# Experts 4 to 7 of a top-1 routed layer in one pass each, by programs of 33 widths

## The chip, the cores and the metric

The kernel runs on one core of one Trainium2 chip. The metric is the device time of one execution in microseconds (us). All arithmetic of the products is in float32.

## The reference

A state-space scan gives 3072 tokens of 256 values; a router sends each token to the expert with the greatest logit, and the expert's two products are scaled by the softmax weight of that logit. Cut to what matters:

```python
x = attn_out.transpose(0, 2, 1, 3).reshape(3072, 256)   # scan over 4 x 8 heads, 768 steps
logits = x @ w_gate                                     # 8 experts
expert_idx = np.argmax(logits, axis=1)
probs = softmax(logits)
gate_w = probs[np.arange(N), expert_idx]
for e in range(8):
    mask = expert_idx == e
    h = np.maximum(x[mask] @ w1[e], 0.0)                # 256 -> 1024
    out[mask] = gate_w[mask, None] * (h @ w2[e])        # 1024 -> 256
```

With the inputs of this case the experts get 372, 343, 418, 417, 336, 365, 415 and 406 tokens.

## The kernel before, in words

**First part.** The scan runs over 24 tiles of 128 tokens. Each tile's rows (values, logits, token number: W = 265 numbers) are kept, and groups of tiles (RGS) are ranked: by counts and a triangular product, every token gets a place in its expert's region of x_hbm, a buffer in HBM. place (L553) scatters a tile to its places with an indirect DMA on GpSimd's queue. Tiles 0 to 16 are placed during the scan. Tiles 17 to 23, the last group, are ranked after it and get places from 256 on at least, so that the first 256 places of an expert may be read before the last group is known. empty (L190) writes zero rows, with a token number that is out of range, behind the tokens of the first groups.

**Second part.** Expert e has two weight matrices of 1 MB each (w_sb). Its first pass handles places 0 to 255: a_load (L596) fetches the rows from x_hbm; halves (L651, L653) splits the float32 words in two planes of 16 bits and turns them with a transposing DMA; words (L658) puts the turned planes together on VectorE into xT; m_h (L685) makes h in eight blocks, each with a ReLU by ScalarE into hT; m_y (L720) makes the result for two tiles of 128 tokens with hT as the stationary operand, and put (L703 by ScalarE, L705 by VectorE) scales it by the gate into yo, which an indirect DMA (L711, GpSimd) sends to its tokens in the output. TensorE's order is h of expert 0, h of 1, y of 0, h of 2, y of 1, and so on, one expert apart.

**What is left of an expert**, its places from 256, is done in pairs of experts: b_load (L606, L609) fetches a full tile of each and half a tile that both share. A Switch with five branches does h for 128 to 192 places according to the greater count of the pair, and m_half (L731) the shared half tile where one is needed. TensorE and ScalarE take the branch by a number that over computes from the counts; switch_hint names the target some time ahead.

**Order.** The program of the second part is recorded in a manual schedule: on each engine the instructions stand in the order in which the Python code emits them. VectorE, ScalarE and GpSimd each take them from one sequence. All fetches of rows and weights, all emptyings and all transposing DMAs are issued by SP from one sequence too: an issue whose wait isn't over holds all behind it. Weights of expert e + 2 are issued in the middle of expert e's first product, after the turn of expert e + 2. Placements and result sends are on GpSimd's queue. Buffers come from rotating pools: y_ps has two PSUM buffers, h_ps four, yo three, hT three.

A general path (If more > 0) serves inputs whose counts go over the places; it isn't taken here.

Of the kernel before, what the change touches and what calls it, by code (L numbers as in the profile page):

```python
# [24 lines left out]
NT = NP * NC  # L25
# [12 lines left out]
TA = CA // 128  # L38
NK = -(-(N - CAP) // 128)
NR = N + 128  # L40
# [4 lines left out]
def ssd_then_moe(ctx, tc, x, ad_in, az_in, B, BT, CT, w_gate, w1, w2, out):  # L45
# [30 lines left out]
    zrows = consts.tile([112, CAP // 112, W], FP32, name="zrows")  # L76
# [13 lines left out]
    nk = route.tile([128, 2 * E + 1 + E // 2], I32, name="nk")  # L90
# [50 lines left out]
    def empty_consts():  # L141

        z = sm.tile([128, 1], FP32, name="zero")
        nc.gpsimd.memset(z, 0.0)
        none_i = sm.tile([112, CAP // 112], I32, name="none_i")
        nc.gpsimd.iota(none_i, pattern=[[0, CAP // 112]], base=N, channel_multiplier=0)
        nc.scalar.copy(zrows, bc(z[0:112, 0:1, None], list(zrows.shape)))
        nc.gpsimd.tensor_copy(zrows[:, :, TOK].bitcast(I32), none_i)
# [37 lines left out]
    def empty(e):  # L186
# [3 lines left out]
        d = nc.sync.dma_start(out=x_hbm[ds(r, CAP), :].rearrange("(p c) w -> p c w", c=CAP // 112), in_=zrows)  # L190
        tc.declare_no_dep(d.ins, group="pa", reason="these rows lie behind the first pass's tokens")
        tc.declare_no_dep(d.ins, group="la", reason="another expert's rows")
        tc.add_to_no_dep_group("fl", d.ins)

# [82 lines left out]
    def load_w(e, uu=(0, 1)):  # L277
        for u in uu:
            nc.sync.dma_start(out=w_sb[e][u], in_=(w1, w2)[u][e])
# [254 lines left out]
    def rank(g):  # L534
# [11 lines left out]
        if g == GA - 1:  # L546
            nc.vector.tensor_tensor(out=row2, in0=rt_p[g][0:1, n], in1=base_f[0:1], op=ALU.add)

            nc.vector.scalar_tensor_tensor(out=base2, in0=rt_p[g][:, n], scalar=float(CA), in1=base_f,
                                           op0=ALU.max, op1=ALU.add)  # L550
# [16 lines left out]
    def over(tb, pp):  # L567
# [6 lines left out]
        nc.vector.tensor_scalar(out=ov, in0=cn, scalar1=float(127 - CAP), scalar2=0.0, op0=ALU.add, op1=ALU.max)  # L574
# [5 lines left out]
        nc.vector.tensor_copy(nk[:, E + 1:2 * E + 1], cn)  # L580

        ml = tb.tile([128, E // 2], FP32, name="ml")
        nc.vector.tensor_reduce(ml, cn.rearrange("p (b i) -> p b i", i=2), axis=AX, op=ALU.max)
        nc.vector.tensor_scalar(out=ml, in0=ml, scalar1=float(15 - CA - 128), scalar2=0.0, op0=ALU.add, op1=ALU.max)
        nc.vector.tensor_scalar(out=ml, in0=ml, scalar1=64.0, scalar2=None, op0=ALU.min)
        cl = nk[:, 2 * E + 1:]
        nc.vector.tensor_copy(cl, ml)
        nc.vector.tensor_scalar(out=cl, in0=cl, scalar1=4, scalar2=None, op0=ALU.logical_shift_right)
# [3 lines left out]
    pr = [dict() for _ in range(E // 2)]  # L592
# [8 lines left out]
    def b_load(v, mo):  # L601
        xs = ea.tile([128, TA, W], FP32, name="xs", bufs=4)
        xh = mo.tile([128, 1, W], FP32, name="xh", bufs=4)
# [8 lines left out]
    def gate_in(xs, n):  # L612

        lg = xs[:, :, 128:HB]
        mx = ea.tile([128, TA], FP32, name="gmx", bufs=2)[:, 0:n]
        nc.vector.tensor_reduce(mx, lg, axis=AX, op=ALU.max)
        sub = ea.tile([128, TA, E], FP32, name="gsub", bufs=2)[:, 0:n]
# [3 lines left out]
    def gate_out(sub, n):  # L621
        nc.scalar.activation(sub, sub, func=ACT.Exp)
        gt = ea.tile([128, TA], FP32, name="gate", bufs=5)[:, 0:n]
# [11 lines left out]
    def new_xT():  # L635
        return ea.tile([128, KT, CA], FP32, name="xT", bufs=3)
# [8 lines left out]
    def halves(tiles):  # L645
        n = len(tiles)
        pl = ea.tile([128, TA + 1, 2, KT, 128], U16, name="pl", bufs=2)[:, 0:n]
# [4 lines left out]
        tt = ea.tile([128, TA + 1, 2, KT, 128], U16, name="plT", bufs=2)[:, 0:n]  # L652
# [7 lines left out]
    def next_halves(i):  # L660

        if i < E:
            ex[i]["tt"] = halves([ex[i]["xs"][:, t] for t in range(TA)])
        elif i - E < E // 2:
            r = pr[i - E]
            r["tt"] = halves([r["xs"][:, 0], r["xs"][:, 1], r["xh"][:, 0]])

    def a_words(e):
        ex[e]["xT"] = new_xT()
        for i in range(TA):  # L670
# [9 lines left out]
    def up(xT, w, f, n, pp, step=CA):  # L680
        p = pp.tile([128, 512], FP32, name="h_ps", tag="h", bufs=4)
        for i in range(0, n, step):
            for t in range(KT):
                c = t * F + f * 128
                nc.tensor.matmul(p[:, i:min(i + step, n)], lhsT=w[:, c:c + 128], rhs=xT[:, t, i:min(i + step, n)],  # L685
# [347 lines left out]
```

## Time and profile before

| | us |
|---|---|
| median of 3 runs | 271.21 (270.74 to 272.68) |
| the profiled execution's own time | 271.81 |
| its span, first to last instruction | 270.0 |
| TensorE busy | 252.9 |
| VectorE, ScalarE, GpSimd busy | 110.7, 104.5, 87.0 |
| first product of expert 0 starts | 83.20 |
| mean granted TensorE clock | 0.992 |

PE is TensorE's products, PEld its weight loads, DVE VectorE, ACT ScalarE, POOL GpSimd; SPq is the issuing of DMAs by SP. L685 is a line of the kernel before. The slices divide the span in 40 equal parts of 6.75 us; a digit is the busy share in tenths. In the chain, an entry is a start, a length and the work; x32 counts TensorE's records, of which a float32 product has two. In timelines, what stands in brackets is how long the engine had been idle and what ended it. Idle time of an engine other than the one that sets the end costs nothing by itself.

The kernel moved 43.57 MB by DMA, 36.32 of them on the queue that SP issues to, 6.41 on GpSimd's.

### The profile page before, as it was taken

Reading aid. Unit: us, or ns where it says so; the run is one execution under the profiler, and the core shown is the slowest. Engines: PE = TensorE matmul, PEld = TensorE weight load, DVE = VectorE, ACT = ScalarE, POOL = GpSimd, SP = SyncE. Lnnn points to the kernel's source line nnn. Section 1 sums busy time; section 2 is a strip of 40 time slices with the busy share of each in tenths; the row PEclk is TensorE's granted clock in tenths of the full one; section 3 lists DMA queues with packets and bytes.
Section 4 is the critical chain, followed back from the end, with each engine's and each line's share of the span. In section 5 each row is a group of like instructions: output and inputs, shape, how many; then the busy total and the mean of one; then the engine's idle time right before and its main releaser. Section 6 shows DMA issues by size and latency. Waiting matters only on the chain.

```text
span 270.0 us, 7603 instructions
## 1 busy us (share of the span) xinstructions
PE 252.9 (94%) x3044; PEld 213.7 (79%) x3067; DVE 110.7 (41%) x358; ACT 104.5 (39%) x304; POOL 87.0 (32%) x171
## 2 busy tenths in 40 slices
PE   8799898999997999999999999999999999999990
PEld 2577677677776888888888888888998978989770
DVE  4889887888854240421211111233225115321010
ACT  6958574655543423223232323141050520604200
POOL 5666875866720002025504120202211102121021
PEclk9999999999999999999999999999999999999996
DMA  6956767671434899949695959533330601401010
GB/s 182 374 172 171 228 199 236 165 247 51 135 118 101 212 367 310 384 177 294 236 256 202 279 199 335 130 91 78 103 85 9 94 4 30 90 6 40 2 35 28
DMA packets 29715, 43.57 MB, mean 161 GB/s; under 512 B 16203, under 2 KB 19917, under 8 KB 27984
## 3 DMA queue, kind: packets, MB, share of 16 engines
q1 hardware_dynamic: 27152, 36.32, 45.4%
q0 software_dynamic: 2496, 6.41, 7.1%
q8 instruction: 36, 0.59, 0.9%
q14 instruction: 31, 0.25, 0.3%
HBM read 29.10 MB, written 10.73 MB: 147 GB/s over the span
## 4 chain that ended last, share of the span: by engine, by line
PE 82%; DVE 5%; DMA 4%; issue 4%; POOL 2%; ACT 1%; POOLq 0%; ACTq 0%; DVEq 0%
PE h_ps L685 33%; PE y_ps L720 30%; PE y L176 5%; PE rows_ps L176 4%; PE g L176 3%; PE A L176 3%; PE yh_ps L731 3%; DVE L L359 2%; DMA x_hbm<-rows,pos 1%; DMA xs<-x_hbm 1%; DMA az<-in_az_dram 1%; DMA ct<-in_CT_dram 1%; DVE M L386 1%; PE rank L176 1%; DVE S L431 1%
## 5 line engine op out<-in xcount | busy, mean ns | idle before, releaser
L685 PE MATMUL h_ps<-xT,w 128*128 128x256 f32 (+3 forms) x516 | 90.3, 334 | 0.6 <-ACT xT L641 0.5
L685 PEld LDWEIGHTS h_ps<-xT,w 128*128 128x128 f32 x516 | 81.3, 190 | 8.2 <-ACT xT L641 0.7
L720 PE MATMUL y_ps<-w,hT 128*128 128x256 f32 x384 | 84.9, 380 | 0.0
L720 PEld LDWEIGHTS y_ps<-w,hT 128*128 128x128 f32 x384 | 72.6, 190 | 10.5 <-issue 0.8
L696 ACT ACTIVATE hT<-h_ps 128x256 f32<-128x256 f32 (+3 forms) x128 | 43.3, 339 | 60.8 <-PE h_ps L685 53.1
L711 POOL DMA_INDIRECT out_dram<-yo,xs x24 | 23.7, 988 | 91.1 <-ACT yo L703 64.7
L553 POOL DMA_INDIRECT x_hbm<-rows,pos x24 | 24.4, 1015 | 20.6 <-DMA x_hbm<-zrows 13.3
L359 DVE TENSOR_TENSOR_SCAN L<-abc,ident 128x512 f32<-128x512 f32 x24 | 29.1, 1213 | 0.0
L651 DVE COPY pl<-xs 128x256 uint16<-128x256 uint16 x44 | 10.4, 298 | 43.8 <-DMA xs<-x_hbm 43.7
L658 DVE COPY xT<-plT 128x512 uint16<-128x512 uint16 (+1 forms) x30 | 10.6, 415 | 33.6 <-DMA plT<-pl 27.8
L703 ACT ACTIVATE yo<-y_ps,gate 128x256 f32<-128x256 f32 x14 | 6.6, 474 | 39.4 <-PE y_ps L720 24.5
L386 DVE TENSOR_TENSOR M<-g,L 128x512 f32<-128x512 f32 x24 | 16.5, 687 | 5.6 <-PE g L176 5.1
L176 PE MATMUL rows_ps<-turn,yT 128*128 128x136 f32 x96 | 15.4, 283 | 3.5 <-issue 2.7
L705 DVE TENSOR_SCALAR yo<-y_ps,gate 128x256 f32<-128x256 f32 x10 | 4.8, 482 | 29.3 <-PE y_ps L720 29.3
L176 PE MATMUL g<-ctm,bt 32*64 32x128 f32 x384 | 16.3, 280 | 0.5 <-ACT ctm L293 0.4
L176 PEld LDWEIGHTS rows_ps<-turn,yT 128*128 128x128 f32 x96 | 14.5, 192 | 1.3 <-issue 0.4
L711 POOL DMA_INDIRECT out_dram<-yh,xh x4 | 3.9, 978 | 35.7 <-ACT yh L733 23.9
L470 ACT COPY rows<-rows_ps 128x264 f32<-128x264 f32 x24 | 9.1, 380 | 13.5 <-PE rows_ps L176 10.9
L176 PE MATMUL y<-M,xn 64*32 64x64 f32 x768 | 12.9, 223 | 1.2 <-issue 1.2
L457 ACT COPY yT<-y 128x256 f32<-128x256 f32 x24 | 8.9, 372 | 12.2 <-PE y L176 10.2
L176 PEld LDWEIGHTS g<-ctm,bt 32*64 32x64 f32 x384 | 10.4, 131 | 3.2 <-ACT ctm L293 0.9
L366 POOL TENSOR_TENSOR bs<-bn,L 128x128 f32<-128x128 f32 x22 | 9.0, 410 | 11.1 <-DVE L L359 10.0
(132 smaller groups left out, 203.3 us busy)
## 6 DMA issues: line engine op xcount, KB each, us to landing
w<-in_w_dram SPq DMA_DIRECT2D x13, 1024.0 KB
x_hbm<-zrows SPq DMA_DIRECT2D x8, 463.8 KB
xn<-in_x_dram SPq DMA_DIRECT2D x12, 256.0 KB
w<-in_w_dram SPq DMA_DIRECT2D x12, 256.0 KB
xs<-x_hbm SPq DMA_DIRECT2D x8, 265.0 KB
ct<-in_CT_dram SPq DMA_DIRECT2D x6, 256.0 KB
bt<-in_BT_dram SPq DMA_DIRECT2D x6, 256.0 KB
bn<-in_B_dram SPq DMA_DIRECT2D x6, 256.0 KB
```

Of the source, the lines that this page charges most:

```text
L176: i = nc.tensor.matmul(out, lhsT=lhsT, rhs=rhs, **kw)
L359: nc.vector.tensor_tensor_scan(out=s["L"].rearrange("p h i -> p (h i)"), data0=s["abc"], data1=ident8.rearrange("p h i -> p (h i)"), initi ...
L366: nc.gpsimd.tensor_tensor(out=bs[n % 2], in0=gr[n // CG]["B"][:, n % CG].rearrange("p (h m) -> p h m", h=8), in1=bc(st[n]["L"][:, :, CH - ...
L386: nc.vector.tensor_tensor(out=s["M"].rearrange("p (s v u) i -> p s v (u i)", s=2, v=2), in0=s["g"][:, :, 0:256].rearrange("p v (s f) -> p ...
L470: nc.scalar.copy(out=rt[g][:, k - R0[g], 0:DM + E], in_=p)
L553: s_ = nc.gpsimd.indirect_dma_start(out=x_hbm[:, :], out_offset=bass.IndirectOffsetOnAxis(ap=pos[:, k:k + 1], axis=0), in_=rt[grp[k]][:, k ...
L651: nc.vector.tensor_copy(pl[:, i, :, t], f[:, :, HB * t:HB * t + 128])
L658: nc.vector.tensor_copy(xT.bitcast(U16).rearrange("p t (j c) -> p c t j", c=2), tt)
L685: nc.tensor.matmul(p[:, i:min(i + step, n)], lhsT=w[:, c:c + 128], rhs=xT[:, t, i:min(i + step, n)], start=(t == 0), stop=(t == KT - 1))
L696: nc.scalar.activation(hT[:, f, 0:n], p, func=ACT.Relu)
L711: s_ = nc.gpsimd.indirect_dma_start(out=out[:, :], out_offset=bass.IndirectOffsetOnAxis(ap=xs[:, TOK:TOK + 1].bitcast(I32), axis=0), in_=y ...
L720: nc.tensor.matmul(p, lhsT=hT[:, f], rhs=w_sb[e][1][:, f * DM:f * DM + DM], start=(f == 0), stop=(f == FT - 1))
```

## The change

Experts 0 to 3 keep a first pass of 256 places and pairs for the rest (EP = 4). Experts 4 to 7 are done in one pass over up to 512 places (CP = 512): a Switch with 33 branches does exactly 256 + 8c places (m_one). In it the second product has w2 as the stationary operand and hT as the moving one, so that the result comes out turned (yTp); turn_back splits it in planes, turns it with a transposing DMA, and put_back puts the words together, scales them and sends four tiles per expert.

So that a program's expert has all its tokens, the last group is ranked, counted and placed during the first product of expert 0 (late); experts 3 to 7 are emptied behind all of their tokens, after the count (empty_last), experts 0 to 2 before it as till now. p_load fetches 512 rows of an expert and waits for all placements and emptyings.

TensorE's order becomes: h of 0, h of 1, y of 0, y of 1, six of eight blocks of h of 2, program of 4, the other two blocks, one tile of y of 2, program of 5, the other tile, two blocks of h of 3, program of 6, the other six blocks, program of 7, y of 3, pair 0, pair 1. The fetch, turn and weights of a program's expert are issued one program ahead. Weights of experts 4 to 7 share two pairs of buffers. The loads of both matrices of expert 3 and of 7 wait for the last product that was emitted before them (behind=True). yo gets four buffers, hT two, xT four; clearing of hT for pairs moves from VectorE to GpSimd.

```diff
+GAP = 3
+EP = 4
+CP = 512
+NCP = (CP - CA) // 8 + 1
...
+    def empty_last(e):
+        r = nc.values_load(nk[0:1, E + 1 + e:E + 2 + e], engines=[ENG.SP], min_val=0, max_val=N, ...)
+        d = nc.sync.dma_start(out=x_hbm[ds(r + e * NR, CP), :].rearrange("(p c) w -> p c w", c=CP // 128), in_=zrows)
...
-    def load_w(e, uu=(0, 1)):
+    def load_w(e, uu=(0, 1), behind=False):
         for u in uu:
-            nc.sync.dma_start(out=w_sb[e][u], in_=(w1, w2)[u][e])
+            d = nc.sync.dma_start(out=w_sb[e][u], in_=(w1, w2)[u][e])
+            if behind:
+                tc.add_manual_dep(d.ins, made[0].ins.name, ...)
...
+    def p_load(e):
+        xs = ea.tile([128, CP // 128, W], FP32, name="xp", bufs=2)
+        nc.sync.dma_start(out=xs, in_=x_hbm[e * NR:e * NR + CP, :].rearrange("(t p) w -> p t w", p=128))
...
-        yo = mo.tile([128, DM], FP32, name="yo", bufs=3)
+        yo = mo.tile([128, DM], FP32, name="yo", bufs=4)
...
+    def m_one(e, hT, yT, n, pp):
+        for f in range(FT):
+            nc.scalar.activation(hT[:, f, 0:n], up(ex[e]["xT"], w_sb[e][0], f, n, pp, CP), func=ACT.Relu)
+        for m in range(KT):
+            p = pp.tile([128, 512], FP32, name="y_ps", tag="y", bufs=2)[:, 0:n]
+            for f in range(FT):
+                c = f * DM + m * 128
+                nc.tensor.matmul(p, lhsT=w_sb[e][1][:, c:c + 128], rhs=hT[:, f, 0:n], ...)
+            nc.scalar.copy(yT[:, m, 0:n], p)
+
+    def turn_back(yT):
+        pl = ea.tile([128, CP // 128, 2, KT, 128], U16, name="pl", bufs=2)
+        f = yT.bitcast(U16).rearrange("p m (j c) -> p c m j", c=2)
+        for i in range(CP // 128):
+            nc.vector.tensor_copy(pl[:, i], f[:, :, :, 128 * i:128 * i + 128])
+        tt = ea.tile([128, CP // 128, 2, KT, 128], U16, name="plT", bufs=2)
+        nc.sync.dma_start_transpose(out=tt..., in_=pl...)
+        return tt
+
+    def put_back(e, tt, mo):
+        for i in range(CP // 128):
+            yo = mo.tile([128, DM], FP32, name="yo", bufs=4)
+            nc.vector.tensor_copy(yo.bitcast(U16).rearrange("p (m j c) -> p c m j", c=2, m=KT), tt[:, i])
+            nc.vector.tensor_scalar(out=yo, in0=yo, scalar1=ex[e]["gate"][:, i:i + 1], ..., op0=ALU.mult)
+            send(yo, ex[e]["xs"][:, i])
...
-                for e in range(2):
+                for e in range(GAP):
                     empty(e)
...
+        def late():
+            g_in(0)
+            load_w(1, (1,))
+            rank_pe(last, rank_ps)
+            rank(last)
+            for k in range(R0[GA], NT):
+                place(k)
+                nc.gpsimd.memset(apart, 0.0)
+            x_words(1)
+            over(tb, pp)
+            for e in range(GAP, E):
+                empty_last(e)
+            x_halves(2)
+            g_in(1)
+            g_in(2)
+            x_words(2)
+            load_w(2, (0,))
+            new_w(EP)
+            load_w(EP, (0,))
+            p_load(EP)
+
+        def one(i):
+            e = EP + i
+            hT = mo.tile([128, FT, CP], FP32, name="hTp", bufs=1)
+            for c in tc.Switch(cls[i], NCP, f"e{e}"):
+                m_one(e, hT, yTp, CA + 8 * c, pp)
+            hint(i + 1)
+            return turn_back(yTp)
+
+        first(0, late)
+        g_out(0)
+        first(1)
+        g_out(1)
+        second(0, pick)
+        x_halves(EP)
+        g_in(EP)
+        load_w(EP, (1,))
+        p_load(EP + 1)
+        load_w(2, (1,))
+        new_w(EP + 1)
+        load_w(EP + 1)
+        hint(0)
+        second(1, pick)
+        x_words(EP)
+        ...
+        first(2, None, range(0, 6))
+        tt = one(0)
+        g_out(EP + 1)
+        first(2, None, range(6, FT))
+        second(2, pick, (0,))
+        load_w(3, (0, 1), True)
+        new_w(EP + 2)
+        load_w(EP + 2)
+        a_load(3)
+        p_load(EP + 2)
+        put_back(EP, tt, mo)
+        x_halves(3)
+        g_in(3)
+        x_words(3)
+        x_halves(EP + 2)
+        g_in(EP + 2)
+        x_words(EP + 2)
+        tt = one(1)
+        ...
+        second(2, pick, (1,))
+        first(3, None, range(0, 2))
+        new_w(EP + 3)
+        load_w(EP + 3, (0, 1), True)
+        put_back(EP + 1, tt, mo)
+        p_load(EP + 3)
+        for v in range(EP // 2):
+            b_load(v, mo)
+        x_halves(EP + 3)
+        g_in(EP + 3)
+        x_words(EP + 3)
+        b_halves(0)
+        b_in(0)
+        b_words(0)
+        tt = one(2)
+        g_out(EP + 3)
+        first(3, None, range(2, FT))
+        put_back(EP + 2, tt, mo)
+        b_halves(1)
+        b_in(1)
+        b_words(1)
+        tt = one(3)
+        for v in range(EP // 2):
+            b_out(v)
+        put_back(EP + 3, tt, mo)
+        second(3)
+        for v in range(EP // 2):
+            pr[v]["hT"] = [new_hT(mo) for _ in range(2)]
+            for h in pr[v]["hT"]:
+                nc.gpsimd.memset(h[:, :, 144:CB], 0.0)
...
```

## The prediction

> **What bounds the kernel now.** I read the page's busy table first, then its slices, then the chain in order of time, then the timelines of the load queue (SP) and of VectorE. Page:
>
> ```profile
> span 270.0 us, 7603 instructions
> PE 252.9 (94%) x3044; PEld 213.7 (79%) x3067; DVE 110.7 (41%) x358; ACT 104.5 (39%) x304; POOL 87.0 (32%) x171
> PE   8799898999997999999999999999999999999990
> DMA  6956767671434899949695959533330601401010
> ```
>
> From slice 13 on TensorE never pauses. The DMA engines are half to nine tenths busy there up to about 170 us, then nearly idle. The chain gives prices (start, us, what):
>
> ```profile
> 83.20 11.68 PE h_ps L685 x56
> ...
> 118.59 6.91 PE h_ps L685 x32
> 125.49 6.91 PE y_ps L720 x32
> ...
> 194.56 7.14 PE h_ps L685 x64
> 201.71 6.91 PE y_ps L720 x32
> 208.61 9.55 PE h_ps L685 x64
> 218.17 3.60 PE yh_ps L731 x32
> ...
> 243.10 8.95 PE h_ps L685 x64
> 252.05 3.60 PE yh_ps L731 x32
> ```
>
> One expert's first pass (256 places) is 6.91 + 6.91 us: 32 records per product, 216 ns each, so 0.844 ns per column and record. A pair's program is 64 records: 7.14 us at 128 columns (6.91 of work, so 0.23 for the jump), 9.55 at 176, 8.95 at 160; the half tile, where there is one, is 3.60. Experts fill 83.2 to 262.8, all of it TensorE work; the tail after it is 7.2 us. The margin that hides everything else shows in the load queue:
>
> ```profile
> 105.80 1.97 SPq L279 DMA_DIRECT2D w<-in_w_dram  x2
> 108.31 1.19 SPq L190 DMA_DIRECT2D x_hbm<-zrows  x2
> 111.52 0.41 SPq L596 DMA_DIRECT2D xs<-x_hbm  x1
> 120.39 1.31 SPq L653 DMA_TRANSPOSE plT<-pl  x1
> ```
>
> ```profile
> 119.46 0.90 DVE L651 COPY pl<-xs 128x256 uint16<-128x256 uint16 x4 [7.27 <-DMA xs<-x_hbm]
> 123.76 0.79 DVE L658 COPY xT<-plT 128x512 uint16<-128x512 uint16 x2 [2.80 <-DMA plT<-pl]
> ```
>
> A fetch of 265 KB issued at 111.5 is there at 119.4, because 2 MB of weights and two row writes stand ahead of it. From fetch to turned operand takes 12.2 us, and the kernel before hides it because that operand is used only at about 132.
>
> **What the Trainium skill says.** "DMA: Bandwidth & Descriptors", Queues, rings and completion order: an engine consumes descriptors of one queue in ring order. The trace agrees (the 8 us above). Same page, Anatomy of one DMA: about 2 us fixed until an indirect transfer counts as landed. The chain has 3.50 us from POOL's start of a placement to its landing, some 2.3 beyond the 1.0 POOL needs. "TensorE: Matmul & The Clock Gate", Architectural detail: ScalarE and VectorE are strict FIFO. No row contradicts it. Same page, Part 1: after an idle window of about 3.4 us the clock falls to half until a busy window has passed. No run here shows it: the clock is 0.992 and TensorE is never idle so long.
>
> **What the products cost.** From the reference's inputs the experts have 372, 343, 418, 417, 336, 365, 415, 406 tokens. Before, experts 4 to 7 cost 4 × 13.82 = 55.3, pair 2 is 7.14 + 6.91 = 14.05, pair 3 is 0.17 + 8.95 + 3.60 + 6.91 = 19.6: 88.9 us. After, the programs take 336, 368, 416 and 408 columns, 64 records each: 64 × 0.844 ns × 1528 = 82.5, plus four jumps of 0.23: 83.4. TensorE has 5.5 us less to do. Wider moving operands are not in the trace; the three widths it has lie on one line, so I take it. ReLU copies (384 ns at 256 columns, 277 at 128, so some 0.55 at 416) stay under TensorE's 1.4 us per block. The new copies, turns and 16 result sends lie on ScalarE, VectorE, POOL and DMA, which have room: nothing by themselves, but their order matters. The clearing of yTp and yh on POOL lies in its pause from 76.6 to 86 and costs nothing; if it ran over, the late placements would start later. The five row writes on SP, 0.66 each to issue (1.3 for two), lie under w2's transfer; else they would move every fetch behind them.
>
> **Start of the experts.** Three emptyings instead of two stand ahead of the first fetch; they were done at 76.2, the fetch waits until 79.07 for the last placement. The third adds 1.2 to 1.9: bound 0 to 0.7, taken 0.3. The count (over) follows the ranks directly in one PSUM buffer: TensorE waits for one VectorE read, 0.45.
>
> **Stall A, ahead of the first program.** Expert 4's fetch stands in the one queue behind expert 2's fetch, w2 of 1, five writes of 543 KB, a turn, w1 of 2 and w1 of 4. Prices from the packets of the trace, as added to a full queue: 1 MB of weights 3.1 to 3.4; a 464 KB write 1.2 (behind weights) to 1.9 (alone), so 1.4 to 2.2 for 543 KB; 256 KB turn 1.3; fetch 1.3 per 265 KB (0.7 to 1.8). From 88.7 (end of expert 1's turn): 1.3 + 3.1 + 5 × 1.44 + 1.5 (seven late placements, 0.93 MB, on POOL's queue beside it; estimate from the 0.8 us that 0.5 MB added at 123 to 131) + 1.3 + 6.3 + 2.6 = 112.0. Landing 0.4, eight plane copies of 0.225 make 114.2, the turn 3.4 (120.36 to 123.76 above) + 1.5 for twice the size, three word copies 1.2: 120.3. TensorE arrives at 83.5 + 0.65 + 27.6 + 5.2 = 117.0. On the way another wait: the gates of expert 0 stand on VectorE behind expert 2's words, which wait for the turn behind those writes (103.5). So gates at 104.9; the ScalarE copy that frees the y buffer at 105.4 against 104.9: 0.5. Start 120.4, against 116.2 if nothing waited: A costs 4.2 in all, the two start terms included. With writes at 2.2 and fetches at their slow ends it is 9.5.
>
> **Stall B, ahead of expert 6.** w1 and w2 of expert 3 now wait for the last product ahead of expert 5's program. Behind these two on SP stand w1 and w2 of 6, fetches of 3 and 6, and two turns. From that product: 1.3 + 4 × 3.14 + 0.8 (four result sends) + 1.3 + 2.6 + 0.4 = 19.0 for the fetch of 6, but its planes stand on VectorE behind expert 3's turn and words: 21.6. Planes 1.85, turn 4.9, words 1.4: 29.7. TensorE has 20.1 + 3.45 + 1.73 = 25.3 to do. B costs 4.4 (3 to 7).
>
> **Stall C, ahead of expert 7.** Its fetch reuses the buffer that expert 5's sends still read. From the start of expert 6's program: turning back expert 5 is 6.4 (planes 1.5, turn 4.9), four result tiles and the fourth send's landing 7.2, so the fetch is issued at 13.6 and there at 18.0; planes 1.9; the pairs' fetches ahead of the turn 2.3; turn 3.5, words 1.5: 27.2. TensorE has 22.7 + 5.2 = 27.9. Taken 0, up to 2.
>
> **Stall D, ahead of pair 0.** Results of expert 3 reuse the first result buffers of expert 7. ScalarE's copy so waits for expert 7's first send to land, and behind it in FIFO stand pair 0's ReLUs. From the end of expert 7's last product: copy 0.7, planes 1.5, turn 4.9, words and gate 0.8, POOL and landing 2.5: 10.4. Two copies and the second send: ReLU done at 12.5. TensorE has 6.91 + 0.23 + four PSUM banks of 0.43 = 8.9: D costs 3.7 (3 to 4.7). In pair 1 the clearing of hT is on POOL behind two sends (2.9 until the first ReLU against 2.6): 0.6.
>
> **Clock.** Gaps of 3 to 4.4 us are at the edge; half clock for some 5 us would cost 2.5, taken 0.7, bound 0 to 4.
>
> **Sum.** −5.5 + 4.2 + 4.4 + 0 + 3.7 + 0.6 + 0.7 = +8.1. The profiled execution's own time is 271.81 (span 270.0 and 1.8 around it), so about 279.9; against the median of 271.21, 279.3. I predict 279.5.
>
> **Rivals.** (1) Not slower: the queue delivers sooner. For: 8 KB packets beside other traffic were moved at up to 411 GB/s (109.4 to 115.9). Against: over 97 to 119 the mean was some 330. It decides where expert 4's fetch lands by 108 and expert 6's within 14.6 us of its product; then A keeps 1.3 (0.3, 0.45 and the gates' 0.5), B goes, the clock holds, and 271.2 − 5.5 + 1.3 + 3.7 + 0.6 = 271.3. Only if D went too would it be faster, 267.6. (2) The queue at its slow ends and the clock fallen: A 9.5, B 7, C 2, D 4.5, clock 4, pair 0.6: 271.2 − 5.5 + 27.6 = 293 if all come together; with a third of the way from the forecast to there left out, 288. For: places and sends cross the queue. Against: DMA is not at its limit at every step. (3) The programs don't get what they promise: 33 targets each, fetched late, at about 2 us per jump (an estimate: two 16 KB instruction packets of 1.0 us each in the trace), 8 more: 287. Against: the pairs' jumps, hinted in the same way, cost 0.23.
>
> **Chances.** Forecast (275 to 284) 0.53; rival 1 0.15; rival 2 0.26; rival 3 0.06. 1% is about what a measurement of this kernel can tell from no change. Faster 0.04, within it 0.11, slower 0.85. The range takes in most of rival 1's upper half and rival 2 to 290.
>
> **What would show it.** TensorE idle 3 us or more just before the first product of expert 4, released by the word copies xTp; again before expert 6; a pause of 3 to 4 us inside pair 0's first product, released by ScalarE, whose copy waits for a result send. Programs at 18.1, 19.9, 22.5 and 22.0 us. I am wrong if the fetch of expert 4 lands before 109 or after 117, if programs don't follow the columns, or if a clock below 0.97 appears.

## The result, and the profile after

The changed kernel takes 292.32 us (median of four runs, 290.44 to 294.1) against 271.53 us of the kernel before on the same chip: a ratio of 1.076, 95% interval 1.068 to 1.084. It is slower, as forecast, but by 20.8 us and not by 8. From the page of the changed kernel, its span, the busy table, TensorE's slices and its clock (other rows left out):

```profile
span 291.2 us, 7230 instructions
PE 257.9 (89%) x2843; PEld 187.7 (64%) x2843; DVE 120.8 (41%) x381; ACT 96.3 (33%) x269; POOL 93.4 (32%) x188
PE   8899999999899989499959994999999992999990
PEclk9999999999999999979999999899999999699997
```

The row of nines of before now has four holes (the 4, 5, 4 and 2 from slice 16 on), and the clock falls just behind three of them. TensorE's table of waits names them (engine, tile, line, releaser, the work whose end let TensorE go on: us in total, times, longest). An "issue" is a pause for which the profile shows no releaser; that of 3.9 us stands ahead of expert 4's program.

```profile
PE h_ps L717 <- ACT hT L728: 5.6, 1, 5.6
PE h_ps L717 <- issue: 4.1, 2, 3.9
PE h_ps L717 <- DVE xTp L691: 3.9, 1, 3.9
PE h_ps L717 <- DVE yo L784: 3.4, 1, 3.4
...
PE y_ps L752 <- ACT yo L735: 1.3, 1, 1.3
```

TensorE's timeline puts them in place (start, us, line, shapes, count of records, and in brackets the pause ahead of the group with its releaser):

```profile
123.74 10.77 PE L717 MATMUL h_ps<-xTp,wp 128*128 128x336 f32 x32 [3.92 <-issue]
134.34 9.20 PE L766 MATMUL y_ps<-hTp,wp 128*128 128x336 f32 x32
...
152.16 10.13 PE L717 MATMUL h_ps<-xTp,wp 128*128 128x368 f32 x32 [3.43 <-DVE yo L784]
162.12 10.06 PE L766 MATMUL y_ps<-hTp,wp 128*128 128x368 f32 x32
...
181.29 13.13 PE L717 MATMUL h_ps<-xTp,wp 128*128 128x416 f32 x32 [3.93 <-DVE xTp L691]
194.27 11.34 PE L766 MATMUL y_ps<-hTp,wp 128*128 128x416 f32 x32
...
210.85 11.12 PE L717 MATMUL h_ps<-xTp,wp 128*128 128x408 f32 x32
221.81 11.12 PE L766 MATMUL y_ps<-hTp,wp 128*128 128x408 f32 x32
...
247.27 8.37 PE L717 MATMUL h_ps<-xT,w 128*128 128x128 f32 x48 [5.64 <-ACT hT L728]
```

The four programs stand here with both products, which have the same number of columns and so should take the same time. They don't behind two of the three pauses: 10.77 against 9.20 for expert 4, 13.13 against 11.34 for expert 6. The windows of the trace show why (window, its length, busy time of PE, PEld, DVE, ACT, POOL, then the granted clock, 1 being full, the DMA share and GB/s):

```profile
124.00:128.00 4.00, 4.00 (x10) 2.51 (x10) 2.38 (x14) 0.69 (x2) 0.00 (x0) 0.66 1.06 418
182.00:186.00 4.00, 4.00 (x9) 2.03 (x8) 1.40 (x8) 0.52 (x1) 0.00 (x0) 0.65 0.64 120
246.00:250.00 4.00, 2.73 (x13) 2.73 (x14) 0.00 (x0) 1.81 (x7) 3.19 (x4) 0.53 0.21 73
```

The clock is 0.66, 0.65 and 0.53 there. The time can be added up. From the first product of an expert to the last, the kernel before takes 179.56 us (83.20 to 262.76), the changed one 199.07 (84.22 to 283.29). I call this the experts' stage. Of its 19.5 us more, pauses are 18.6 (18.78 against 0.17), and slow clock is 6.3: 1.6 and 1.8 at the programs of 4 and 6, 2.9 in pair 0 (8.37 for 48 records, which take 5.48 at the rate of the 64 in 7.31 us of before). That leaves −5.4 for the products themselves: the gain is there, as forecast. The rest of the 21.2 us by which the span grew is a start 1.0 later and a tail 0.7 longer. Below, times are medians of all runs, while ratios leave out runs more than 1.5% above the fastest of their kernel (one of e6_all took 415 us); the profiled runs of e4_gate, e7_fill, e9_xp and e11_h5 are among those left out.

### The profile page after: what moved, and what is told of

Read it like the earlier page. It is cut to its first block, busy times and chain, and to the rows that moved or that the text cites. A ratio compares the mean times of both kernels' runs of the same rounds, so it can differ in the third digit from the quotient of the medians.

```text
span 291.2 us, 7230 instructions
## 1 busy us (share of the span) xinstructions
PE 257.9 (89%) x2843; PEld 187.7 (64%) x2843; DVE 120.8 (41%) x381; ACT 96.3 (33%) x269; POOL 93.4 (32%) x188
## 4 chain that ended last, share of the span: by engine, by line
PE 43%; issue 33%; DMA 9%; POOL 5%; DVE 4%; SPq 2%; ACT 1%; POOLq 0%; ACTq 0%; DVEq 0%
PE h_ps L717 12%; PE y_ps L752 6%; PE y L180 6%; DMA plT<-pl 6%; PE g L180 5%; POOL out_dram L743 4%; PE A L180 3%; PE y_ps L766 3%; PE rows_ps L180 3%; PE abc L180 2%; PE wake_ps L180 2%; DMA x_hbm<-rows,pos 1%; DVE L L381 1%; DMA xs<-x_hbm 1%; PE yh_ps L792 1%
## 5 line engine op out<-in xcount | busy, mean ns | idle before, releaser
L717 PE MATMUL h_ps<-xTp,wp 128*128 128x336 f32 (+3 forms) x128 | 45.2, 514 | 11.3 <-DVE xTp L691 3.9
L717 PE MATMUL h_ps<-xT,w 128*128 128x256 f32 (+2 forms) x260 | 49.3, 351 | 6.3 <-ACT hT L728 5.6
L717 PEld LDWEIGHTS h_ps<-xT,w 128*128 128x128 f32 x260 | 43.8, 205 | 11.2 <-ACT hT L728 6.4
L717 PEld LDWEIGHTS h_ps<-xTp,wp 128*128 128x128 f32 x128 | 25.7, 203 | 29.8 <-issue 15.7
L752 PE MATMUL y_ps<-w,hT 128*128 128x256 f32 x192 | 42.8, 380 | 1.3 <-ACT yo L735 1.3
L766 PE MATMUL y_ps<-hTp,wp 128*128 128x336 f32 (+3 forms) x128 | 41.7, 484 | 0.0
L752 PEld LDWEIGHTS y_ps<-w,hT 128*128 128x128 f32 x192 | 36.2, 190 | 7.3 <-ACT yo L735 1.7
L743 POOL DMA_INDIRECT out_dram<-yo,xp x16 | 16.5, 1028 | 62.2 <-DVE yo L784 60.1
L766 PEld LDWEIGHTS y_ps<-hTp,wp 128*128 128x128 f32 x128 | 24.3, 190 | 16.7 <-issue 10.0
L728 ACT ACTIVATE hT<-h_ps 128x256 f32<-128x256 f32 (+2 forms) x64 | 20.1, 340 | 31.6 <-PE h_ps L717 28.1
```

The lines of the kernel that those rows point to most:

```text
L717: made[0] = nc.tensor.matmul(p[:, i:min(i + step, n)], lhsT=w[:, c:c + 128], rhs=xT[:, t, i:min(i + step, n)], start=(t == 0), stop=(t == ...
L728: nc.scalar.activation(hT[:, f, 0:n], p, func=ACT.Relu)
L743: s_ = nc.gpsimd.indirect_dma_start(out=out[:, :], out_offset=bass.IndirectOffsetOnAxis(ap=xs[:, TOK:TOK + 1].bitcast(I32), axis=0), in_=y ...
L752: made[0] = nc.tensor.matmul(p, lhsT=hT[:, f], rhs=w_sb[e][1][:, f * DM:f * DM + DM], start=(f == 0), stop=(f == FT - 1))
L766: nc.tensor.matmul(p, lhsT=w_sb[e][1][:, c:c + 128], rhs=hT[:, f, 0:n], start=(f == 0), stop=(f == FT - 1))
```

## The experiments

The experts' stage is compared beside the time, because the time of one kernel spreads by 1 to 3% from run to run. Much of that lies ahead of the stage: over the profiled runs the stage starts anywhere from 80.9 to 86.4 us, although nothing ahead of it is edited (in e3_fetch, e5_jump and e11_h5 TensorE's clock was 0.58, 0.60 and 0.58 from 78 to 86 us). "Before" is the kernel before on the same chip; no ratio is given where the runs spread too far for one, or where there was one run. Pauses are those ahead of, or early inside, the programs of 4, 5, 6, 7 and pair 0; the wait inside expert 0's second product, second(0), of 0 to 2.5 us, is not among them. A turn is a transposing DMA, and "the words of 6" are VectorE's copies that put expert 6's turned words together, the last step ahead of its program. Each trace is one execution.

| kernel | time, us | before, us | ratio (95%) | stage, us | pauses at 4 / 5 / 6 / 7 / pair 0 |
|---|---|---|---|---|---|
| before | 271.53 | | | 179.56 | none |
| changed | 292.32 | 271.53 | 1.076 (1.068–1.084) | 199.07 | 3.9 / 3.4 / 3.9 / 0 / 5.6 |
| e1_yo6 | 283.10 | 272.12 | 1.033 (1.025–1.041) | 191.26 | 4.2 / 3.5 / 0.5 / 2.4 / 0 |
| e2_w3 | 290.28 | 272.12 | 1.069 (1.061–1.077) | 194.53 | 1.4 / 3.5 / 0 / 0 / 5.6 |
| e3_fetch | 288.15 | 272.12 | 1.057 (1.049–1.064) | 194.02 | 1.5 / 3.5 / 0 / 2.2 / 5.6 |
| e4_gate | 289.15 | 269.65 | 1.066 (1.052–1.079) | 198.79 | 6.1 / 3.4 / 0.4 / 2.1 / 5.6 |
| e5_jump | 291.58 | 272.12 | | 194.40 | 2.1 / 0.7 / 4.6 / 0.2 / 5.6 |
| e7_fill | 295.67 | 269.65 | | 204.39 | filled / 3.6 / filled / 2.3 / 4.6 |
| e8_nojump | 283.38 | 269.65 | 1.054 (1.046–1.063) | 191.13 | 0.8 / 0 / 4.8 / 0 / 5.0 |
| e9_xp | 289.11 | 271.65 | | 194.60 | 2.9 / 3.4 / 0 / 0 / 5.6 |
| e13_fill5 | 289.07 | 269.25 | | 197.65 | 3.9 / filled / 0.4 / 0 / 5.6 |
| e6_all | 272.36 | 269.65 | 1.006 (1.003–1.010) | 182.17 | 1.4 / 1.1 / 3.2 / 0 / 0 |
| e10_xp3 | 273.80 | 271.65 | 1.003 (1.000–1.006) | 179.15 | 1.4 / 0.8 / 0 / 0.6 / 0.3 |
| e11_h5 | 272.03 | 271.65 | 0.999 (0.997–1.002) | 177.49 | 0.5 / 1.4 / 0.2 / 0 / 0 |
| e12_best | 266.06 | 269.25 | 0.989 (0.984–0.994) | 175.95 | 0 / 1.8 / 0 / 0.3 / 0 |

**Result buffers (e1_yo6).** The edit, in put and in put_back:

```diff
-        yo = mo.tile([128, DM], FP32, name="yo", bufs=4)
+        yo = mo.tile([128, DM], FP32, name="yo", bufs=6)
```

> Six result buffers (yo) in place of four, nothing else. Theory: the 5.64 us pause inside pair 0's first products and the half clock behind it (its 48 records 8.37 us in place of 5.2) come from ScalarE, whose copy of expert 3's first tile waits for a buffer that program 7's sends still hold; with six the copy takes a buffer sent long before. Then the pause is under 1 us, the 48 records take 5.2 to 5.6 us, and the whole is about 8.8 us shorter: 283.5 against 292.3. Rival: the turn back of program 7 and GpSimd's sends hold TensorE whatever buffer is free; then the pause stays within 1 us of 5.6 and the time within 0.5%.

Measured: ratio 1.033, 283.1 us. On ScalarE's timeline of the changed kernel the two copies of expert 3 wait for result sends of program 7, and pair 0's ReLUs stand behind them:

```profile
244.78 0.47 ACT L735 ACTIVATE yo<-y_ps,gate 128x256 f32<-128x256 f32 x1 [8.49 <-DMA out_dram<-yo,xp]
246.20 0.47 ACT L735 ACTIVATE yo<-y_ps,gate 128x256 f32<-128x256 f32 x1 [0.94 <-DMA out_dram<-yo,xp]
246.94 0.79 ACT L728 ACTIVATE hT<-h_ps 128x128 f32<-128x128 f32 x4 [0.26 <-issue]
```

With six buffers neither waits for a send, the first not at all (ScalarE again), and TensorE runs the 64 records in one piece:

```profile
235.56 0.47 ACT L735 ACTIVATE yo<-y_ps,gate 128x256 f32<-128x256 f32 x1
239.01 0.47 ACT L735 ACTIVATE yo<-y_ps,gate 128x256 f32<-128x256 f32 x1 [2.98 <-PE y_ps L752]
```

```profile
238.81 7.48 PE L717 MATMUL h_ps<-xT,w 128*128 128x128 f32 x64
```

So the pause and the slow clock at pair 0 are the reuse of result buffers; the rival falls. That the time came out at the figure expected is partly chance. The pause before 6 went too, while 2.4 us of new pause stand ahead of the program of 7 and the first product of 5 fell into slow clock (11.69 us in place of 10.13).

**The hold on expert 3's weights (e2_w3).**

```diff
-        load_w(3, (0, 1), True)
+        load_w(3)
```

> The weights of expert 3 are not held behind the product of expert 2 any more; expert 7's still are. Theory: the 3.93 us pause before the program of 6 and its slow first product (13.13 us in place of 11.3) come from the fetch of 6 queued behind a 4 MB burst that could start only at 149.7; with the burst from about 138 the fetch of 6 lands some 8 us sooner, the pause goes, the clock stays full: about 5.6 us shorter, 286.7. Rival: the fetch of 6 waits for program 4's sends whatever the weights do; then the pause stays at 3 us or more. On the pause of 3.43 us before the program of 5: if the burst of weights delayed the jump's instructions, it goes too (283.3); if the jump's own fetch and the short lead of TensorE's sequencer make it, it stays within 1 us.

Measured: ratio 1.069, which the intervals do not tell from the change's 1.076; in the trace the pause before 6 is gone, the one before 5 is 3.50. The reason expected was wrong. The weights were issued only 3.05 us sooner (145.71 in place of 148.76), not ten: on SP's queue program 4's turn back stands ahead of them, so the hold was worth 3 us on top of a wait that was there anyway. And the pause before 6 proves to have little behind it. The words of 6 begin at 173.7 here; in the changed kernel they begin at 179.8, because the turns of 3 and 6 took 2.8 and 3.8 us in place of the 1.5 and 2.6 of this run, and the burst came 3 us later. TensorE arrives at 177 to 179. In e1_yo6, e3_fetch and e13_fill5, whose order here is that of the change, the words begin at 175.0 to 176.6 and the pause ahead is zero. This kernel's pause before 6 is a margin of a few us, crossed or not.

**The fetch of expert 4 (e3_fetch).**

```diff
+            p_load(EP)
             load_w(2, (0,))
             new_w(EP)
             load_w(EP, (0,))
-            p_load(EP)
```

> The fetch of expert 4 is queued ahead of the 2 MB of weights of experts 2 and 4, which before stood ahead of it. Theory: the 3.92 us pause before the program of 4 is this queueing (weights 104.7 to 112.1, fetch 110.0 to 114.2); with the fetch first it lands near 109, the words are ready near 117, before TensorE reaches the program at 119.8: the pause and the slow clock behind it go, 3.9 + 1.7 = 5.6 us, 286.7. Rival: the fetch is held by the row writes ahead of it and by the placements, not by the weights; then it lands no sooner than 112 and the pause stays at 2 us or more, and the weights of 4, now later, add to it.

Measured: ratio 1.057. The fetch landed at 112.05, which is 25.7 us after the start of the experts; in the changed kernel it landed 30.0 after. But the words came only 2 us sooner (36.3 against 38.3 after the start), because 2 MB of weights now ran beside the turn, which took 4.3 us in place of 2.7. And 35.6 to 38.7 is what eight traces with the change's own order here give, the changed kernel's among them; the pause before 4 moves between 0 and 4 us from run to run. The ratio is clear of the change's (1.057 against 1.076), but the one trace does not show that this edit is the cause: the pause before 6, which it does not touch, is gone there too.

**Expert 0's gates (e4_gate).**

```diff
             x_words(1)
+            g_out(0)
             over(tb, pp)
...
         first(0, late)
-        g_out(0)
```

> Expert 0's gates are put on VectorE's queue ahead of the turned words of expert 2 and not behind them. Theory: the 1.30 us in which TensorE waited at the second half of second(0) for ScalarE's scaled tile is these gates queued behind words that wait for a turn; now the wait is under 0.3 us, but the pause before the program of 4, whose end the fetch sets, grows by as much: time within 1% of the change's 292.3. Rival: the fetch is not what sets that pause; then it stays at 3.9 and the whole is 1.3 us shorter.

Measured: the wait at second(0) is zero in place of 1.30, and the two pauses at the program of 4 are 1.70 and 4.38 in place of 3.92: the stage is 198.79 against 199.07. Of the 2.2 us that these pauses grew, 1.3 are the wait taken off; 0.8 are words of 4 that came later after the start (39.1 against 38.3). This agrees with the theory, that a wait ahead of a longer wait is worth nothing by itself; one trace, in which the pause before 6 shrank as well, does not prove it.

**Where the jump stands (e5_jump).**

```diff
-        first(2, None, range(0, 6))
+        first(2, None, range(0, FT))
         tt = one(0)
         g_out(EP + 1)
-        first(2, None, range(6, FT))
         second(2, pick, (0,))
```

> Expert 2's last two blocks of the first product (2.6 us with what lies around them) stand before the program of 4 in place of behind it, so that between the programs of 4 and 5 there is only one second product, and it waits for no ReLU of ScalarE. Theory: the 3.43 us pause before the program of 5 is a jump that takes about 4 us because its target was not there, reached by TensorE's sequencer only 1 us ahead of TensorE, since the second product's last matmuls waited for late ReLUs; with these done long before, the sequencer reaches the jump about 3 us ahead and the pause falls under 1.2 us. The pause before the program of 4 shrinks by the work moved ahead of it, to 1.0 to 1.8, with no slow clock behind it. In all 6 to 7 us shorter, 285.5 to 286.5. Rival: the burst of weights that starts behind the second product holds up the fetch of the jump's instructions; then the pause before 5 stays at 3 us or more, and only the 4.3 us before program 4 are gained (288).

The trace records what TensorE's sequencer does. In the changed kernel, between the programs of 4 and 5 (start, us, record; the profile counts none of these as busy; a hint names the jump's target ahead of time, the compare-and-branch is the jump):

```
139.154 0.036 BRANCH_PREFETCH_HINT
147.743 4.150 COMPARE_BRANCH
151.951 0.040 BRANCH_PREFETCH_HINT
```

The jump took 4.15 us and was reached 1.0 us before TensorE ran dry at 148.73: the last matmuls of second(2) had waited for ReLUs that ScalarE, itself 2.6 us on its way out of the program of 4, gave at 147.4. The profile puts the pause down to a VectorE copy of result words, which happened to end then. In e5_jump the jump still took 3.33 us, but TensorE had work:

```profile
144.98 3.62 PE L752 MATMUL y_ps<-w,hT 128*128 128x256 f32 x16
148.43 5.11 PE L717 MATMUL h_ps<-xTp,wp 128*128 128x368 f32 x16
```

The rival, weights that hold the instructions up, falls: here the jump was over at 148.03, before the weights were issued at 148.98, and was slow all the same. But of the 6 to 7 us expected the stage gained 4.7, and the time hardly moved (four runs of 287.62 to 293.54): the pause before 6 was 4.6, since TensorE came earlier, and a new one of 2.07 stands inside the program of 4, released by ReLUs. Those are ScalarE's own jump: it reached the jump at 125.0 and began the first ReLU of the program at 130.8, while the four PSUM tiles that TensorE can fill in the meantime are 4.7 us of its work. In the changed kernel the same 5.5 us (120.05 to 125.55) lay under the pause before 4.

**Filled pauses (e7_fill).** Ahead of the programs of 4 and 6:

```diff
+        def busy(n):
+            p = pp.tile([128, 512], FP32, name="y_ps", tag="y", bufs=2)[:, 0:CA]
+            for k in range(n):
+                nc.tensor.matmul(p, lhsT=w_sb[1][0][:, 0:128], rhs=ex[2]["xT"][:, 0, 0:CA],
+                                 start=(k == 0), stop=(k == n - 1))
...
+            if i in (0, 2):
+                busy(17)
```

> 17 matmuls of 128 x 256 whose results nobody reads (3.6 us) are added on TensorE directly ahead of the programs of 4 and 6, where it paused 3.9 us each time. Theory: the clock falls because TensorE was idle, so now the first products of these programs take 9.1 and 11.3 us in place of 10.8 and 13.1, and the added work costs nothing since the operand comes no sooner: 3.4 us shorter, 288.9. Rival: the clock falls for another reason (the restart of large products together with 4 MB transfers); then the products stay slow and the time stays at 292.3 or above.

Each matmul is two records, so the filling was 7.5 us at each place and not 3.6. The time is therefore not what was expected; the rows that decide are:

```profile
118.40 7.50 PE L1036 MATMUL y_ps<-xT,w 128*128 128x256 f32 x34
125.74 9.20 PE L717 MATMUL h_ps<-xTp,wp 128*128 128x336 f32 x32
134.78 9.20 PE L766 MATMUL y_ps<-hTp,wp 128*128 128x336 f32 x32
...
186.82 11.34 PE L717 MATMUL h_ps<-xTp,wp 128*128 128x416 f32 x32
```

First products at the second ones' time, beside transfers at 394 and 375 GB/s (125.5 to 130, 186.5 to 191), against 418 and 120 behind the pauses of the changed kernel: the slow clock is the pause's, and the rival falls.

**No choice of program (e8_nojump).** Experts 4 to 7 with fixed widths; the choice by the counts is left out:

```diff
-            for c in tc.Switch(cls[i], NCP, f"e{e}"):
-                m_one(e, hT, yTp, CA + 8 * c, pp)
+            m_one(e, hT, yTp, (336, 368, 416, 408)[i], pp)
```

> Experts 4 to 7 run without a choice among programs: their widths 336, 368, 416, 408 are fixed in the code, so neither TensorE nor ScalarE jumps there; only the pairs still choose. Left out: the choice by the counts. Theory: the pause of 3.43 us before the program of 5 goes (under 0.8 us) and with it no other pause longer than 1 us, so 3 to 4 us shorter, 288.5; those before 4 and 6 (transfers) and inside pair 0 (result buffers) stay, the first two longer by what arrives sooner. Rival: the pause before 5 is the operand or the weights of 5, late by 3 us; then it stays, and the jumps were worth nothing (292).

Measured: no pause before 5, 4.8 before 6, 5.0 in pair 0; the stage is 7.9 us shorter, twice what was expected. 3.4 of this is the jump; 4.6 are the pause before 4 and its slow clock, most of which did not come in this run (words 36.3 us after the start, see e3_fetch). The other differences (second(0), 6, pair 0) nearly cancel.

**A lead for the jump (e13_fill5).** The same filling ahead of the program of 5 alone.

> 34 matmul records of 128 x 256 whose results nobody reads (7.5 us) are added on TensorE directly ahead of the program of 5, nothing else. Theory: the jump there is slow because it comes 8.6 us after its hint; 7 us later it takes under 0.6 us, as the jump to 6 did when it came 13.6 us after its hint, and the pause of 3.4 us is gone, so the whole is about 4 us longer. Rival: the hint never fetches this program's target; then the jump still takes over 3 us, though hidden behind the added work, and the time is the same 4 us longer. The length of the jump decides, not the time.

Measured: the jump took 0.31 us, 13.1 us after its hint, and TensorE went on without a pause:

```profile
146.62 7.50 PE L1036 MATMUL y_ps<-xT,w 128*128 128x256 f32 x34
153.95 10.06 PE L717 MATMUL h_ps<-xTp,wp 128*128 128x368 f32 x32
```

So this jump can be quick where it comes later after its hint, and the rival falls. But the lead alone does not decide. In the changed kernel jumps came 15.1, 9.7 and 8.65 us after their hints and took 0.44, 0.30 and 0.29 us; others came 8.59, 6.15 and 3.76 after and took 4.15, 3.81 and 3.79; and in e12_best one came 5.4 after and took 0.39. Over the fifteen traces the lead sorts 81 of TensorE's 84 jumps into a program: all that came 8.63 us or more after their hint took at most 1.43, those that came up to 8.59 after it 3.05 to 5.10, but for three (4.84 and 6.68 in the kernel before, 5.44 in e12_best). The leads close to that edge belong to two jumps only, to 5 and to pair 0, so what tells the jumps apart stays open.

**The early fetch of 6 (e9_xp), and everything together (e6_all, e10_xp3, e11_h5, e12_best).** e9_xp is the changed kernel with:

```diff
-        xs = ea.tile([128, CP // 128, W], FP32, name="xp", bufs=2)
+        xs = mo.tile([128, CP // 128, W], FP32, name="xp", bufs=3)
...
         g_in(EP + 1)
+        a_load(3)
+        p_load(EP + 2)
         x_words(EP + 1)
...
-        a_load(3)
-        p_load(EP + 2)
         put_back(EP, tt, mo)
```

> A third buffer for the programs' fetches, so that the fetch of 6 needn't wait until program 4's results are sent, and the fetches of 3 and 6 are issued ahead of program 4's turn back and of the 4 MB of weights of 3 and 6. The weights stay held as in the change. Theory: the pause of 3.93 us before the program of 6 and the 1.8 us of slow clock behind it come from a fetch that could be issued only at 165.3, after the sends and the weights; now it lands before 145, the turn of 6 is over near 172, before TensorE gets there at 177: the pause is under 0.5 us and the whole 5.7 us shorter, 286.6. Rival: the turns of 3 and 6 are queued behind the same 4 MB and come no sooner; then the pause stays at 2.5 us or more.

Measured: no pause before 6, words at 173.0. As e2_w3 shows, that pause goes without this edit too, so the run alone decides nothing. e6_all joins e1, e3, e4 and e5 and issues load_w(3) unheld ahead of x_words(EP + 1):

> Everything together: six result buffers; the fetch of 4 ahead of the weights of 2 and 4; the weights of expert 3 unheld and issued ahead of program 4's turn back; expert 0's gates ahead of the words of 2; expert 2's first product wholly ahead of the program of 4. Theory: the pauses before 4, 5, 6, inside pair 0 and at the gates go, with the slow clock behind them; what is left is the late start (1.0), the wait for cn (0.4), the tail (0.8) and ScalarE's own jumps, which with the other pauses gone hold TensorE some 5 us in sum (2.1 at 4, 0.7 at 5, 2.4 at 7): 7.5 us above a kernel without pauses, less the 5.5 us of products: 273.5 against 271.5 of before. Rival: the pauses move on to the next transfer; then 278 or more.

Measured: 272.36 us, ratio 1.006, as the theory says; but the terms differ. Of ScalarE's jumps 2.5 us are left and not 5, and the pause before 6 came back, 3.2 with 1.8 of slow clock, since TensorE now arrives at 166.5. e10_xp3 adds e9's edit, with expert 3's planes and turn ahead of second(2):

> The kernel with everything together, and this third buffer with the early fetches of 3 and 6. Theory: of what that kernel still loses the pause before 6 (3.23 us) and its slow clock (1.8) go: 5.0 us less, ratio to before 0.988 (0.980 to 0.995). Rival: the pause moves to the next turn or to ScalarE's jump there (some 2 us): ratio 0.995 to 1.003.

Here the early fetch, with expert 3's turn moved beside it, is told from chance. The words of 6 begin at 159.1 in place of 168.2, and TensorE, there at 169.2, goes on at once at full clock (11.4 for the first product in place of 13.1); the stage is 3.0 shorter. The ratio, 1.003, is at the rival's end, and its interval overlaps that of e6_all: new waits of 0.8 at the program of 5 and 0.6 at pair 1 take part of the gain. e11_h5 (where the general path, not taken here, gives up a PSUM buffer for it):

```diff
-        p = pp.tile([128, 512], FP32, name="h_ps", tag="h", bufs=4)
+        p = pp.tile([128, 512], FP32, name="h_ps", tag="h", bufs=5)
```

> As the one before it, with five PSUM tiles for the first products in place of four. Theory: the two waits of 1.40 and 1.13 us inside the first products of the programs of 4 and 5 are TensorE out of free tiles while ScalarE is still on its way into the program; a fifth tile is 1.1 to 1.4 us more of work: both waits go to under 0.3 us, 2 us shorter than with four, ratio to before 0.980. Rival: the wait isn't for tiles; then no difference (within 0.5%).

The wait inside the program of 4 fell from 1.2 to 0.5, as the theory says; the one inside 5, 1.1 in e6_all, was already gone in e10_xp3. The stage is 1.7 shorter, of which these 0.7 are the tiles' and the rest is moves of other waits. The ratio, 0.999, is the rival's: the jumps to 5 and to pair 1 now show 1.4 and 1.3. e12_best:

```diff
-        second(2, pick, (0,))
+        second(2, pick, (0, 1))
...
-        second(2, pick, (1,))
-        first(3, None, range(0, 2))
+        first(3, None, range(0, 5))
...
-        first(3, None, range(2, FT))
+        first(3, None, range(5, FT))
```

> The kernel with all edits and five PSUM tiles, and both tiles of expert 2's second product between the programs of 4 and 5, five of the eight blocks of expert 3's first product between those of 5 and 6. Theory: the 1.42 us ahead of the program of 5 there is the jump of some 3.4 us reached less than 3 us ahead; with 3.6 us more work behind the hint and ahead of the jump it goes: 1.4 us shorter, ratio to before 0.994 (0.988 to 0.999). Rival: expert 3's operands or ScalarE's way out of program 5 are late for the blocks moved ahead; then a pause of 1 us or more stands there and nothing is gained (0.997 to 1.003).

Measured: 266.06 us against 269.25, ratio 0.989 (0.984 to 0.994): 1.1% faster than the kernel before. The step from e11_h5 was 1.5 us of stage, as expected, but not where expected. The jump to 5 took 5.1 us and still shows as 1.8; the waits at 4 and at pair 1 went. TensorE's table of waits has as its longest in the experts' stage this line, the jump again put down to a VectorE row:

```profile
PE h_ps L717 <- DVE gsub L651: 1.8, 1, 1.8
```

Without its 2.5 us of pauses the stage is 173.5, against 179.4 of the kernel before: the 5.5 us that the products were to save, and a little more.

## Why the prediction was wrong

The sign was right, at 0.85; the time, 279.5 with a range to 290, was too low by 13 us. By its own steps:

- **Products, −5.5.** Right: −5.4 in the sum above. The programs took 20.0 and 22.1 us where the clock was full throughout (5 and 7), as forecast (19.9, 22.0).
- **Start of the experts, 0.3.** 1.0 was measured, but starts spread by 5 us from run to run, so nothing follows. The wait for cn, the count, is 0.38 (0.45).
- **Stall A, 4.2 with these two.** Undersized: 6.6 together. The gates cost 1.30 (0.5) and the pause 3.92 (about 3). The five writes took 9.66 us with the late placements beside them (8.7), the weights 7.45 (6.3). Over six traces with this order the pause goes from 0 to 4.2, so the 3 taken was a fair middle and this trace is near the top.
- **Stall B, 4.4.** 3.93 in this trace, by the transfers named. But as a fixed cost the step was wrong: the operand is ready between 175 and 180 and TensorE comes between 177 and 179, so the same order gives 0 in other runs. And the hold was only 3 us of it, since program 4's turn back on SP, not looked at in the forecast, lets the weights start hardly sooner.
- **Stall C, 0.** Right.
- **Stall D, 3.7.** Right in mechanism, shown by e1_yo6; undersized by 1.9. From the end of program 7 TensorE's first freed tile took 14.3 us and not 12.5: the turn 6.0 in place of 4.9, each send some 0.4 longer.
- **Pair 1, 0.6.** 0.18.
- **Clock, 0.7 of at most 4.** This is the term that failed most: 6.3. The forecast took gaps of 3 to 4.4 us as the edge and said that no run showed the fall; the end of the trace of before does show it (TensorE idle from 262.76, clock 0.50 from 265.85). Its own sign of being wrong, a clock below 0.97, came in three of the four runs (0.957 to 0.964). "TensorE: Matmul & The Clock Gate", Part 1 of the Trainium skill, names an idle window of about 3.4 us and calls it free-running, which the forecast left out. The traces agree and tell more. In each of them the clock steps only at times that lie whole multiples of 3.41 us apart. Cut along these times, the changed kernel around its pauses before 4 and 5 (columns as above: window, length, five busy times, clock, DMA share, GB/s):

```profile
119.92:123.33 3.41, 0.00 (x0) 0.00 (x0) 0.82 (x3) 0.32 (x1) 0.00 (x0) 1.00 1.00 310
123.33:126.74 3.41, 3.00 (x6) 1.92 (x7) 1.79 (x10) 0.39 (x1) 0.00 (x0) 0.50 1.04 398
...
147.22:150.64 3.42, 1.51 (x7) 0.97 (x6) 0.73 (x4) 0.68 (x2) 0.65 (x1) 1.00 1.11 172
150.64:154.05 3.41, 1.89 (x6) 1.25 (x7) 2.00 (x5) 0.32 (x1) 2.47 (x3) 1.00 0.95 353
154.05:157.46 3.41, 3.41 (x12) 2.09 (x11) 0.00 (x0) 1.19 (x4) 0.99 (x1) 1.00 0.99 377
```

  and e2_w3 around its wait of 1.99 us at second(0):

```profile
104.56:107.97 3.41, 1.42 (x7) 0.94 (x6) 1.58 (x8) 0.71 (x2) 0.00 (x0) 1.00 1.01 384
107.97:111.39 3.42, 3.42 (x9) 2.71 (x10) 0.00 (x0) 0.16 (x1) 1.99 (x2) 0.50 1.02 391
```

  In the experts' stage of the fifteen traces the clock fell 25 times, always behind such a window in which TensorE had been idle for 1.99 us or more; behind all 760 windows at full clock with 1.95 us idle or less it stayed. The 3.43 us before 5 lay 1.91 us in one window and 1.52 in the next, and nothing fell; that was luck, for six other traces have a pause of 3.4 to 3.6 us in this place and all six show the fall (first product of 5 at 11.60 to 12.87). Each fall lasts 3.41 us, which costs up to 1.7 of work; where TensorE was idle for 1.06 us or more of that window too, as in pair 0, the half clock went on for another. So the expected cost of a pause near 3 us was about 1.7 us, not a fraction of it.
- **The jump to the program of 5, 3.43.** Not in the sum at all. The forecast priced jumps at 0.23, from those of the pairs, where TensorE has 3.5 to 3.8 us of products queued ahead; rival 3 named the mechanism, but as an even 2 us per jump, and gave it 0.06. What counts is the length of the jump less the work queued when the sequencer gets there. Jumps of 3.1, 3.8 and 3.9 us stand in the trace of the kernel before too, reached 3.5 to 3.8 us ahead: all that is seen of them is a pause of 0.17 ahead of pair 3 (the third is the last branch, behind all products). The Trainium skill, "Runtime: NRT & Kernel Launch", Instruction fetch mechanics, says that a taken branch whose target isn't among the two 16 KiB pages held has to fetch it first. The trace agrees in this: 1.7 us after the slow jump began, one 16 KB packet came (149.48 to 150.47), and at 151.9 the sequencer went on. That ScalarE pays as much or more (5.5 us into the program of 4) was not seen either; it shows only once the pauses above it are gone.
- **A reading.** A placement's landing comes 2.5 us (3.50 less 1.01) after POOL's part of it, not 2.3; nothing in the sum rests on it.

Rival 2, slow queues and a fallen clock, gave 288 to 293 and had 0.26: the time is where it put it, but of its terms only the clock came, and its slow queues did not (A 6.6 in place of 9.5, B 3.9 of 7, C 0 of 2). The span grew by 13.1 us more than the sum (21.2 against 8.1): the clock is 5.6 of this, the jump, which no sum had, 3.4, A with the start 2.4, D 1.9 and the tail 0.7; B and pair 1 were 0.9 too high.

## What to carry to other kernels

A pause is priced with what it does to TensorE's clock: near 3 us it mostly costs 1.7 us more, at 2 us it can, and split over two windows one of 3.4 need not. A choice among programs costs nothing only while every engine that takes part reaches its jump with as much work still queued as the jump can take (here up to 5.1 us on TensorE, 5.8 on ScalarE), so count the work between the last wait and the jump, on the engine that feeds TensorE too. Stalls hide one another, and taking one off brings up the next: of this change's, single edits gave back up to 4%, all of them with a new order of the products turned 7.6% slower into 1.1% faster.

## What the runs showed that was not expected

- A jump into a program takes 0.3 to 1.4 us on TensorE or 3.1 to 5.1, hinted each time, and the hint's lead sorts most of them but not all (0.39 at 5.4 us, 4.15 at 8.59). The last branch, which has no hint, took 3.4 to 4.0 in every trace.
- TensorE's clock is decided window by window: 1.95 us of idleness in one of 3.41 left it full, 1.99 halved it for the next.
- A 512 KB turn takes 2.6 us or 3.8 in the same place of the program (that of 6); with 2 MB of weights running beside it, that of 4 took 4.3. Where a transfer is to land just ahead of its use, such a difference can decide between no pause and 4 us with a slow clock behind it.
- The releaser that the profile names for a pause made by a jump is whatever ended last (a result word in the change, a gate in e11_h5, a gate's difference in e12_best). The sequencer's own records had to be read to see it.
